# Grouped-query attention over a cache: reordering two pairs' outputs together, loading small rows of wo ahead of the last V block, and halving two loads of wo

## The chip, the cores and the metric

The kernel runs on one core of one Trainium2 chip. The metric is the time on the device in microseconds (us), as the median of several executions. Most executions of this program lie within 0.3 us of each other on a quiet chip. A *span* is the length of the one execution that the profiler recorded, from its first instruction to its last; it is a little shorter than the time. A run is called slow when it is over 1.5% above the fastest of the same kernel; verdicts use the other runs, called fast.

Engines are named as in the profile: PE (TensorE), DVE (VectorE), ACT (ScalarE), POOL (GpSimd), SP (the queue that issues the loads). A load *lands* when its data has arrived; the trace records sixteen landings for a full load, and a reader waits for the last of them. The *granted clock* is the share of PE's full clock that the profile shows as given to it.

## The reference, cut to what matters

```python
B, Sq, D = 8, 4, 512
Hq, Hkv, Sk, Dh = 32, 8, 2048, 128           # bf16 throughout
q = (x @ wq).reshape(B, Sq, Hq, Dh).transpose(0, 2, 1, 3)
k = repeat(k_cache, 4, axis=1); v = repeat(v_cache, 4, axis=1)
p = softmax(einsum("bhqd,bhkd->bhqk", q, k) * Dh ** -0.5)
o = einsum("bhqk,bhkd->bhqd", p, v)
return o.transpose(0, 2, 1, 3).reshape(B, Sq, Hq * Dh) @ wo
```

K and V are 32 MB each (in units of 1024 KB), wq and wo 4 MB each. Every byte is read once and used little, so the kernel is a stream of loads with matmuls beside it.

## The kernel before

The 8 heads of the cache are taken in four *pairs* (p = 0 to 3). A pair and a batch element make a *unit*: one K block and one V block of 1024 KB. All loads go through one queue in a fixed order, and the last ones are V block 31 and then most of wo:

```python
        if step == NH - 1 - 2 * VB:
            assert not loads                              # K and V are all issued
            nc.sync.dma_start(wo_n[:, :], wo[HP * 128 - 32 : HP * 128, :])   # 32 KB, pair 0
            load_wo_m()                                   # 512 KB, pair 0
            load_wo(1, 0, WR)                             # 1024 KB, pair 1
            load_wo(2, 0, WR)                             # 1024 KB, pair 2
            load_wo(3, 0, 4)                              # 512 KB, pair 3
            load_wo(3, 4, 2)                              # 256 KB
            load_wo(3, 6, 2)                              # 256 KB
```

The output of a pair lies with head dimension on partitions. To be multiplied by wo, it is turned in two steps, each (for pairs 1 to 3) of eight transposes on PE and an eviction, which is a copy of PE's result out of its psum tile, on DVE: `to_tokens(p)`, then `to_wo_rows(p)`. Pairs 0 to 2 are turned during the next pair's work; pair 3 can only be turned after V block 31. The end of the kernel is

```python
    to_tokens(3)
    project(0, 0, WM + 1)      # 10 matmuls of 256 columns
    to_wo_rows(3)
    project(1, 0, WR)          # 16 matmuls
    project(2, 0, WR)          # 16
    project(3, 0, 4)           # 8
    project(3, 4, 2)           # 4
    project(3, 6, 2)           # 4
    # ... ACT evicts half 0 of the output, DVE adds to half 1, two transfers store them
```

`project` runs over half 0 of the columns, then over half 1.

The softmax here doesn't subtract the row's maximum and nothing guards it: scores larger than these inputs give would overflow.

## Time and profile before

| | before |
|---|---|
| time, median (range, runs) | 189.90 us (189.82 to 190.06, 4) |
| span of the profiled execution | 187.7 us (its time was 189.51) |
| busy: PE, DVE, ACT | 85%, 61%, 46% of the span |
| share of the DMA engines' time in the queue of loads | 96.0% |
| read from memory | 75.53 MB, 403 GB/s over the span |

The lines that carry the argument stand in the prediction below. One more is the stretch of 1 us in which PE has nothing to do before the last V block lands (columns: stretch, its length, then busy time of PE, PE's weight loads, DVE, ACT and POOL with the number of instructions, the granted PE clock, the DMA share, GB/s).

```profile
174.00:175.00 1.00, 0.00 (x0) 0.00 (x0) 0.97 (x2) 0.00 (x0) 0.00 (x0) 1.00 1.04 426
```

PE is idle, DVE works on the norms of the last block, and the DMA engines are full.

### The profile page before, as it was taken

The page shows a single profiled execution, that of the slowest core. Times are in us where ns is not written, and L with a number is a line of the kernel's source. Part 1 is how long each engine was busy: PE and PEld are TensorE (multiplying, and loading weights), DVE is VectorE, ACT ScalarE, POOL GpSimd, SP SyncE. Part 2 cuts the span into 40 slices and gives each one's busy share as a digit, 9 for nine tenths or more (in the row PEclk, how much of TensorE's full clock was granted, in tenths as well). Part 3 has the DMA queues.
Part 4 walks back from the last instruction along what each step waited for, and adds up shares of the span by engine and source line. Part 5 has one row for each costly group of instructions (what it writes and reads, how often), then busy time and mean ns, then how long its engine had stood idle before and what let it go on. Part 6 is the DMA issues. An engine that isn't in the chain of part 4 may idle for free.

```text
span 187.7 us, 6524 instructions
## 1 busy us (share of the span) xinstructions
PE 159.3 (85%) x2931; PEld 142.2 (76%) x2931; DVE 113.7 (61%) x220; ACT 86.2 (46%) x170; POOL 6.3 (3%) x9
## 2 busy tenths in 40 slices
PE   0525697799999998999989999999888899999793
PEld 0515397699999898889877887899777789886482
DVE  0580544577777676767665666667666667667400
ACT  2012546665655664435545553546555544453000
POOL 8400000000000000000000000000000000000000
PEclk9995769999999999999999999999999999999999
DMA  6999999999999999999999999999999999999960
GB/s 209 461 447 382 423 436 418 429 425 426 420 424 421 419 431 421 419 436 419 422 429 421 424 429 419 424 421 428 424 424 426 422 428 424 421 429 417 413 271 8
DMA packets 10524, 75.99 MB, mean 405 GB/s; under 512 B 1240, under 2 KB 1368, under 8 KB 1880
## 3 DMA queue, kind: packets, MB, share of 16 engines
q1 hardware_dynamic: 10448, 75.55, 96.0%
q8 instruction: 23, 0.38, 0.7%
q14 instruction: 5, 0.04, 0.1%
q10 hardware_dynamic: 48, 0.02, 0.0%
HBM read 75.53 MB, written 0.03 MB: 403 GB/s over the span
## 4 chain that ended last, share of the span: by engine, by line
DMA 92%; issue 3%; PE 2%; POOL 0%; SPq 0%; DVE 0%; POOLq 0%
DMA k_sb<-in_k_cache_dram 62%; DMA wo_e<-in_wo_dram 13%; DMA wo_sb<-in_wo_dram 9%; DMA v_sb<-in_v_cache_dram 8%; PE out_e L371 1%; PE out_ps L371 1%; DVE out_sb L430 0%; SPq L107 0%; POOL ident masks.py:197 0%; POOL ident masks.py:199 0%; SPq L127 0%; POOL wo_e L164 0%; POOLq masks.py:199 0%; POOLq L447 0%
## 5 line engine op out<-in xcount | busy, mean ns | idle before, releaser
L188 PE MATMUL kp<-ident,k_sb 128*128 128x128 f32 x512 | 82.9, 288 | 14.6 <-POOL ident masks.py:199 7.0
L195 DVE COPY kt<-kp 128x1024 bf16<-128x1024 bf16 x96 | 65.2, 683 | 24.4 <-PE kp L188 23.9
L259 ACT ACTIVATE probs<-s_ps 64x256 bf16<-64x256 f32 x128 | 48.3, 378 | 66.6 <-PE s_ps L249 65.7
L188 PEld LDWEIGHTS kp<-ident,k_sb 128*128 128x128 f32 x512 | 55.9, 144 | 18.0 <-POOL ident masks.py:199 7.0
L249 PE MATMUL s_ps<-q_bd,kt 128*128 128x64 bf16 x1024 | 42.3, 194 | 3.0 <-ACT kt L193 1.9
L249 PEld LDWEIGHTS <-kt 128*128 128x128 bf16 x1024 | 39.9, 99 | 4.7 <-ACT kt L193 2.2
L273 PEld LDWEIGHTS <-v_sb 128*128 128x128 bf16 x1024 | 34.4, 96 | 9.4 <-DMA v_sb<-in_v_cache_dram 2.0
L193 ACT COPY kt<-kp 128x1024 bf16<-128x1024 bf16 x32 | 32.4, 1012 | 12.1 <-PE kp L188 11.4
L273 PE MATMUL o_ps<-probs,v_sb 128*128 128x32 bf16 x1024 | 35.0, 176 | 1.1 <-DMA v_sb<-in_v_cache_dram 1.0
L295 DVE TENSOR_REDUCE l_sb<-l_ps 128x32 f32<-128x512 f32 x32 | 22.1, 691 | 20.1 <-PE l_ps L287 20.0
L287 PE MATMUL l_ps<-probs,ones 128*128 128x512 bf16 x64 | 19.0, 379 | 0.0
L299 DVE RECIPROCAL r_sb<-l_sb 128x32 f32<-128x32 f32 x32 | 11.3, 353 | 1.1
L304 DVE TENSOR_TENSOR oT_all<-o_ps,r_sb 128x32 bf16<-128x32 f32 x32 | 5.8, 181 | 1.9 <-PE o_ps L273 1.6
L429 ACT CAST out_sb<-out_e 32x256 bf16<-32x256 f32 x1 | 0.4, 361 | 13.5 <-PE out_e L371 13.5
L287 PEld LDWEIGHTS <-ones 128*128 128x128 bf16 x64 | 6.1, 98 | 0.4
L236 DVE CAST q_bd<-pse 64x512 bf16<-64x512 f32 x4 | 2.6, 678 | 4.6 <-PE pse L227 4.6
L371 PEld LDWEIGHTS <-oP 128*32 128x32 bf16 x48 | 4.6, 97 | 1.0 <-issue 0.4
L164 POOL MEMSET wo_e<- 64x6144 bf16 x1 | 5.2, 5211 | 0.3 <-POOLq L447 0.3
L171 DVE COPY pick<-ident 128x64 bf16<-128x64 bf16 x4 | 0.6, 220 | 6.5 <-POOL ident masks.py:199 6.5
L356 PE MATMUL out_e<-wo_e,oE 64*32 64x256 bf16 x24 | 4.0, 272 | 0.0
L212 PE MATMUL psq<-xT_sb,wq_sb 128*128 128x32 bf16 x128 | 3.6, 188 | 0.3 <-DVE xT_sb L206 0.3
L212 PEld LDWEIGHTS <-wq_sb 128*128 128x128 bf16 x128 | 3.6, 104 | 0.3 <-issue 0.3
(43 smaller groups left out, 41.2 us busy)
## 6 DMA issues: line engine op xcount, KB each, us to landing
k_sb<-in_k_cache_dram SPq DMA_DIRECT2D x32, 1024.0 KB, 19.5
v_sb<-in_v_cache_dram SPq DMA_DIRECT2D x32, 1024.0 KB, 19.5
wq_sb<-in_wq_dram SPq DMA_DIRECT2D x1, 4096.0 KB, 14.3
wo_sb<-in_wo_dram SPq DMA_DIRECT2D x2, 1024.0 KB, 16.0
wo_m<-in_wo_dram SPq DMA_DIRECT2D x1, 512.0 KB
wo_sb<-in_wo_dram SPq DMA_DIRECT2D x1, 512.0 KB
wo_sb<-in_wo_dram SPq DMA_DIRECT2D x2, 256.0 KB
wo_e<-in_wo_dram SPq DMA_DIRECT2D x8, 60.0 KB
```

The source lines that it names most:

```text
L188: nc.tensor.transpose(kp[:, j, :], k4[:, w : w + 128], ident4[:, :])
L193: nc.scalar.copy(out=kt2, in_=kp2)
L195: nc.vector.tensor_copy(out=kt2, in_=kp2)
L212: nc.tensor.matmul(psq[:, h, :], lhsT=wq_sb[:, r, hh * 128 : (hh + 1) * 128], rhs=xT_sb[:, r, :], start=(r == 0), stop=(r == R - 1),)
L249: nc.tensor.matmul(s_ps[:, 2 * j : 2 * j + 2, :], lhsT=k_t[:, j % (HC // 4), :, e], rhs=q_bd[:, p, e, b, :, :], start=(e == 0), stop=(e == 1),
L259: nc.scalar.activation(out=pr[rows, hf * HC : (hf + 1) * HC, cols], in_=s_ps[rows, :, cols], func=EXP)
L273: nc.tensor.matmul(o_ps[u][:, :], lhsT=vs[u][:, cc, :], rhs=pr[:, cc, :], start=(cc == 0), stop=(cc == C - 1),)
L287: nc.tensor.matmul(l_ps[:, :, :], lhsT=ones[:, :], rhs=pr[:, c : c + LC, :], start=(c == 0), stop=(c + LC == C),)
L295: nc.vector.tensor_reduce(out=l_sb[:, :], in_=l_ps[:, :, :].rearrange("d c q -> d q c"), axis=AX, op=ADD)
L299: nc.vector.reciprocal(r_sb[:, :], l_sb[:, :])
L304: nc.vector.tensor_tensor(out=oT_all[:, p * HP : (p + 1) * HP, b, :], in0=o_ps[u][:, :].rearrange("d (h s) -> d h s", h=HP), in1=r_sbs[u][ ...
L371: nc.tensor.matmul(out_ps[half], lhsT=o, rhs=w[:, half * DH : (half + 1) * DH], start=(half == 1 and p == 0 and r == 0), stop=(p == G2 - 1 ...
```

## The change

Its intent is to shorten the end: PE should have less to do after the last V block, and start on the pieces of wo sooner. It has four parts.

1. Pairs 1 and 2 are turned together, once, instead of one after the other (64 rows instead of twice 32). Pair 0's turning loses some transposes too.
2. wo_n and wo_m, the last rows of pair 0, are loaded ahead of V block 31, and `project(0, ...)` runs three steps before the end.
3. Pairs 1 and 2 of wo are loaded and projected in halves.
4. `project` takes half 1 first, and DVE and ACT, with their stores, change order.

Core of the diff (cuts marked ...):

```diff
+        if u == NU + 2:
+            loads.append(("m", 0))                 # wo_n and wo_m, ahead of the last V block
...
     def project(p, r0, n):
-        for half in range(2):
+        for half in (1, 0):
...
-            elif p > 0 and b == 1:
-                to_tokens(p - 1)
-            elif p > 0 and b == 2:
-                to_wo_rows(p - 1)
+            elif p in (1, 3) and b == 1:
+                to_tokens(p // 2)                  # group 0: pair 0; group 1: pairs 1 and 2
+            elif p in (1, 3) and b == 2:
+                to_wo_rows(p // 2)
...
-            nc.sync.dma_start(wo_n[:, :], wo[HP * 128 - 32 : HP * 128, :])
-            load_wo_m()
-            load_wo(1, 0, WR)
-            load_wo(2, 0, WR)
+            load_wo(1, 0, 4)
+            load_wo(1, 4, 4)
+            load_wo(2, 0, 4)
+            load_wo(2, 4, 4)
...
+        if step == NH - 3:
+            out_ps = [...]
+            project(0, 0, WM + 1)
+
-    to_tokens(3)
-    project(0, 0, WM + 1)
-    to_wo_rows(3)
-    project(1, 0, WR)
-    project(2, 0, WR)
+    to_tokens(2)                                   # group 2: pair 3
+    project(1, 0, 4)
+    to_wo_rows(2)
+    project(1, 4, 4)
+    project(2, 0, 4)
+    project(2, 4, 4)
...
+    nc.vector.tensor_tensor(out=out_sb[1][:, :], in0=out_ps[1], in1=early[:, :], op=ADD)
     nc.scalar.copy(out=out_sb[0][:, :], in_=out_ps[0])
-    nc.vector.tensor_tensor(out=out_sb[1][:, :], in0=out_ps[1], in1=early[:, :], op=ADD)
+    nc.sync.dma_start(out=o2[:, DH:], in_=out_sb[1][:, :])
     nc.scalar.dma_start(out=o2[:, :DH], in_=out_sb[0][:, :])
-    nc.sync.dma_start(out=o2[:, DH:], in_=out_sb[1][:, :])
```

More of the change, by code (lines that the diff above doesn't have):

```diff
@@ L85 @@
     ident4 = const.tile([128, 128], FP32, name="ident4")
-    oT_all = const.tile([128, Hq, B, Sq], BF16, name="oT_all")
+    groups = [(0,), (1, 2), (3,)]
+    oT = [const.tile([128, HP, len(ps), B, Sq], BF16, name=f"oT{ps[0]}") for ps in groups]
     out_sb = [const.tile([T, DH], BF16, name=f"out_sb{i}") for i in range(2)]
-    oP = [None] + [const.tile([128, WR, T], BF16, name=f"oP{p}") for p in range(1, G2)]
+    oP12 = const.tile([128, WR, 2, T], BF16, name="oP12")
+    nat_sb = const.tile([2 * T, HP * 128 + 288], BF16, name="nat_sb")
+    oP3 = const.tile([128, WR, T], BF16, name="oP3")
+    oP = [None, oP12[:, :, 0, :], oP12[:, :, 1, :], oP3[:, :, :]]
     oE = const.tile([64, WE, T], BF16, name="oE")
@@ L94 @@
     ones = const.tile([128, 128], BF16, name="ones")
-    pad = const.tile([128, 96], BF16, name="pad")
+    pad = const.tile([128, 64], BF16, name="pad")
     probs = [const.tile([128, C, NQ], BF16, name=f"probs{i}") for i in range(L // 2 + 2)]
@@ L129, in load_wo_m @@
     def load_wo_m():
+        nc.sync.dma_start(wo_n[:, :], wo[HP * 128 - 32 : HP * 128, :])
         nc.sync.dma_start(
@@ L154, in load_ready @@
             kind, u = loads[-1]
-            if kind == "e":
+            if kind in "em":
                 loads.pop()
-                load_wo_e(u)
+                load_wo_e(u) if kind == "e" else load_wo_m()
                 continue
@@ L223 @@
         )
-    for p in range(G2):
-        pse = psum_s.tile([128, 2, B, NQ], FP32, tag="s", name="pse")
+    for pp in range(0, G2, 2):
         for e in range(2):
+            pse = psum_s.tile([128, 2, B, NQ], FP32, tag="s", name="pse")
             nc.tensor.matmul(
-                pse[:, e, :, :],
+                pse[:, :, :, :],
                 lhsT=pick[:, e, :, :],
-                rhs=qT_all[:, p, :, :, :].rearrange("d b h s -> d (b h s)"),
+                rhs=qT_all[:, pp : pp + 2, :, :, :].rearrange("d p b h s -> d (p b h s)"),
                 start=True,
@@ L233 @@
             )
-        for g in range(2):
-            rows = slice(g * 64, (g + 1) * 64)
-            (nc.scalar.copy if g else nc.vector.tensor_copy)(
-                out=q_bd[rows, p, :, :, g, :], in_=pse[rows, :, :, :]
-            )
+            for g in range(2):
+                rows = slice(g * 64, (g + 1) * 64)
+                (nc.scalar.copy if g else nc.vector.tensor_copy)(
+                    out=q_bd[rows, pp : pp + 2, e, :, g, :], in_=pse[rows, :, :, :]
+                )
     wo_sb = wpool.tile([128, G2 - 1, WR, D], BF16, tag="w", name="wo_sb")
@@ L304, in finish @@
         nc.vector.tensor_tensor(
-            out=oT_all[:, p * HP : (p + 1) * HP, b, :],
+            out=oT[(p + 1) // 2][:, :, (p == 2) * 1, b, :],
             in0=o_ps[u][:, :].rearrange("d (h s) -> d h s", h=HP),
@@ L311, with to_tokens @@
     nats = {}
-    def to_tokens(p):
-        nat = psum_l.tile([T, HP, 128], BF16, tag="l", name="nat")
+    def to_tokens(n):
+        rows = len(groups[n]) * T
+        nat = psum_l.tile([rows, HP, 128], BF16, tag="l", name="nat")
         for h in range(HP):
             nc.tensor.transpose(
-                nat[:, h, :],
-                oT_all[:, p * HP + h, :, :].rearrange("d b s -> d (b s)"),
-                ident[:, :],
-            )
-        nat_sb = small.tile([T, HP * 128 // WR, WR], BF16, tag="nat_sb", name="nat_sb")
+                nat[:, h, :], oT[n][:, h, :, :, :].rearrange("d p b s -> d (p b s)"), ident[:, :]
+            )
+        flat = nat[:, :, :].rearrange("t h d -> t (h d)")
+        nats[n] = nat_sb[:rows, : HP * 128 + (n == 0) * 288]
+        if n > 0:
+            nc.vector.tensor_copy(out=nats[n][:, :], in_=flat)
+            return
+        w = 32 * WE
+        nc.vector.tensor_copy(out=nats[0][:, :w], in_=flat[:, :w])
@@ L322, in to_tokens @@
         nc.vector.tensor_copy(
-            out=nat_sb[:, :, :].rearrange("t q r -> t (q r)"),
-            in_=nat[:, :, :].rearrange("t h d -> t (h d)"),
-        )
-        nats[p] = nat_sb
-    def to_wo_rows(p):
-        flat = nats[p][:, :, :].rearrange("t q r -> t (q r)")
-        if p > 0:
-            perm = psum_l.tile([128, WR, T], BF16, tag="l", name="perm")
-            rows = flat.rearrange("t (q r) -> t r q", r=WR)
+            out=nats[0][:, w : 2 * w], in_=flat[:, NE // 2 * WE : NE // 2 * WE + w]
+        )
@@ L333, in to_wo_rows @@
+        nc.vector.tensor_copy(out=nats[0][:, 2 * w :], in_=flat[:, NE * WE :])
+    def to_wo_rows(n):
+        rows = len(groups[n]) * T
+        if n > 0:
+            perm = psum_l.tile([128, WR, rows], BF16, tag="l", name="perm")
+            by_row = nats[n][:, :].rearrange("t (q r) -> t r q", r=WR)
             for r in range(WR):
-                nc.tensor.transpose(perm[:, r, :], rows[:, r, :], ident[:T, :T])
-            nc.vector.tensor_copy(out=oP[p][:, :, :], in_=perm[:, :, :])
+                nc.tensor.transpose(perm[:, r, :], by_row[:, r, :], ident[:rows, :rows])
+            to = oP3[:, :, :] if n == 2 else oP12[:, :, :, :].rearrange("q r p t -> q r (p t)")
+            nc.vector.tensor_copy(out=to, in_=perm[:, :, :])
@@ L336, in to_wo_rows @@
             return
         perm = psum_l.tile([128, WE + WM + 1, T], BF16, tag="l", name="perm")
-        rows = flat[:, : NE * WE + 12 * WE].rearrange("t (q r) -> t r q", r=WE)
+        w = 64 * WE
+        by_row = nats[0][:, :w].rearrange("t (q r) -> t r q", r=WE)
         for r in range(WE):
-            for hi in range(2):
-                q0 = hi * NE // 2
-                nc.tensor.transpose(
-                    perm[hi * 32 : hi * 32 + 32, r, :], rows[:, r, q0 : q0 + 32], ident[:T, :T]
-                )
@@ L346, in to_wo_rows @@
-        rows = flat[:, NE * WE : HP * 128 - 32].rearrange("t (q r) -> t r q", r=WM)
+            nc.tensor.transpose(perm[:64, r, :], by_row[:, r, :], ident[:T, :T])
+        by_row = nats[0][:, w : w + 128 * WM].rearrange("t (q r) -> t r q", r=WM)
         for r in range(WM):
-            nc.tensor.transpose(perm[:, WE + r, :], rows[:, r, :], ident[:T, :T])
-        nc.tensor.transpose(perm[:32, WE + WM, :], flat[:, HP * 128 - 32 :], ident[:T, :T])
+            nc.tensor.transpose(perm[:, WE + r, :], by_row[:, r, :], ident[:T, :T])
@@ L350, in to_wo_rows @@
+        nc.tensor.transpose(perm[:32, WE + WM, :], nats[0][:, w + 128 * WM :], ident[:T, :T])
         nc.vector.tensor_copy(out=oN[:, :], in_=perm[:32, WE + WM, :])
@@ L364, in project @@
     def project(p, r0, n):
-        for half in range(2):
+        for half in (1, 0):
             for r in range(r0, r0 + n):
                 if p > 0:
-                    o, w = oP[p][:, r, :], wo_sb[:, p - 1, r]
+                    o, w = oP[p][:, r], wo_sb[:, p - 1, r]
                 else:
@@ L417 @@
             nc.vector.tensor_copy(out=early[:, :], in_=out_e[:, 1, :])
-    out_ps = [out_e[:, 0, :], psum_s.tile([T, DH], FP32, tag="s", name="out_ps")[:, :]]
-    to_tokens(3)
-    project(0, 0, WM + 1)
-    to_wo_rows(3)
-    project(1, 0, WR)
-    project(2, 0, WR)
+        if step == NH - 3:
+            out_ps = [out_e[:, 0, :], psum_s.tile([T, DH], FP32, tag="s", name="out_ps")[:, :]]
+            project(0, 0, WM + 1)
[5 more added lines that the diff above has]
+    project(2, 4, 4)
     project(3, 0, 4)
```

## The prediction

> **What bounds the kernel now.** I read the page's slices first, to see which resource is full and where it stops being full.
>
> ```profile
> PE   0525697799999998999989999999888899999793
> DMA  6999999999999999999999999999999999999960
> GB/s 209 461 447 382 423 436 418 429 425 426 420 424 421 419 431 421 419 436 419 422 429 421 424 429 419 424 421 428 424 424 426 422 428 424 421 429 417 413 271 8
> ```
>
> From the second slice to the 38th the DMA engines are full at about 424 GB/s, whatever the compute engines do. 75.5 MB must be read from memory, and 75.5 MB / 424 GB/s is 178 us of the 187.7 us span. So work on TensorE (PE) or VectorE (DVE) that is taken out of the middle is worth nothing; only the stretch in which the DMA row falls, the last 5% of the span, can pay. Next I read the chain of work that ended last, from the place where it enters that stretch:
>
> ```profile
> 165.00 16.04 DMA wo_sb<-in_wo_dram
> 181.04 0.04 issue
> 181.08 1.03 PE out_e L371 x8
> 182.12 0.87 PE out_ps L371 x8
> 182.99 0.44 PE out_e L371 x4
> 183.43 0.44 PE out_ps L371 x4
> 183.86 0.22 PE out_e L371 x2
> 184.08 0.22 PE out_ps L371 x2
> 184.30 0.22 PE out_e L371 x2
> 184.52 0.23 PE out_ps L371 x2
> 184.75 0.02 issue
> 184.77 0.41 DVE out_sb L430
> ```
>
> The chain leaves the DMA at 181.04, when pair 2's quarter of wo, one transfer of 1024 KB, has landed whole. From there PE runs 32 matmuls without a pause until 184.75. Three smaller pieces of pair 3 landed meanwhile and no wait shows for them: PE was behind. The 32 matmuls start between 181.08 and 184.55, so one takes 3.47/32 = 0.1085 us in the stream (the 0.27 us that a record shows is its latency). Last I read busy time and DMA share by stretches of 1 us, to see when data really ends (columns: stretch, its length, five engines busy, granted clock, DMA share, GB/s):
>
> ```profile
> 177.00:178.00 1.00, 1.00 (x9) 0.61 (x9) 0.59 (x1) 0.00 (x0) 0.00 (x0) 1.00 1.03 428
> 178.00:179.00 1.00, 1.00 (x13) 0.76 (x11) 0.00 (x0) 0.00 (x0) 0.00 (x0) 1.00 0.81 340
> 181.00:182.00 1.00, 0.92 (x9) 0.81 (x9) 0.00 (x0) 0.00 (x0) 0.00 (x0) 1.00 0.66 256
> 182.00:183.00 1.00, 1.00 (x12) 0.89 (x10) 0.00 (x0) 0.00 (x0) 0.00 (x0) 1.00 0.39 137
> 183.00:184.00 1.00, 1.00 (x11) 0.89 (x10) 0.00 (x0) 0.00 (x0) 0.00 (x0) 1.00 0.02 6
> ```
>
> Some DMA engines run dry at 178 (share 0.81, 13 of 16), the slowest near 183.6, so the finish is uneven. The trace also records the sixteen landings of every transfer. I group them by transfer and take the last of each: block 30 of V at 172.44, block 31 (the last) at 174.99, wo_n 175.20, wo_m 176.24, pair 1 at 178.63, pair 2 at 181.06, and pair 3's pieces (512, 256, 256 KB) at 182.33, 182.97 and 183.59. All are on one queue in this order.
>
> **What the Trainium skill says.**
> 1. "DMA: Bandwidth & Descriptors", "Why a DMA increments its semaphore by 16 and not by 1": a transfer is spread over up to 16 engines that finish independently, and only the full count means that all has landed. The trace agrees: the last piece's sixteen landings run from 178.31 to 183.59, and pair 2's 16 matmuls start at 181.08, after its last landing at 181.06. So a reader waits for the slowest engine on the whole transfer, and halving a transfer lets half the reading start earlier.
> 2. Same page, "Measured (HBM→SBUF, 128 partitions, SWDGE, issued from GpSimd)": 1 MB alone gets 78% of peak, and its rule asks for 1 MiB or more. That speaks against halves. It is for transfers by themselves on another issue path; behind one another on a full queue this trace shows no such cost. Averaged over the sixteen engines, 1024 KB (pair 2) took 2.44 us after the transfer before it, 512 KB 1.22, and the 256 KB pieces 0.63 each.
> 3. "TensorE: Matmul & The Clock Gate", "Back-to-back issue gap": N/2.4 + 2.5 ns warm, for N = 256 that is 109 ns. The trace's 108.5 ns agrees, so this tail already runs at PE's rate, with the granted clock at 1.00, and can be shortened only by starting earlier.
>
> **The change part by part.**
> *Pairs 1 and 2 reordered together.* The order of instructions in both kernels shows 32 fewer matmul instructions in the changed one: 16 transposes (two groups of 8 go), 12 in pair 0's reordering (one transpose in place of two for each of 12 rows), and 4 matmuls of 512 columns in place of 8 of 256 in the setup. At 0.1 us or so that is about 3 us of PE. All of it lies before 160 us, where the DMA share is 1.01 in the stretches of 40 us that I read: 0 on the path. Two VectorE evictions go, and pair 0's copy becomes three: also 0.
>
> *Rows of pair 0 (wo_n, wo_m) ahead of the last V block.* 32 + 512 KB on the queue take 176.24 - 174.99 = 1.25 us. The last V block therefore lands at 176.24 instead of 174.99, and nothing behind it moves. Pair 0's 10 projection matmuls, which lay at 176.8 to 178.3 between the last V block and the end, now run in the pause in which PE waited for that block (PE busy 0.00 from 174 to 175). They wait for wo_m (172.44 + 1.25 = 173.69) and take about 1.1: done at 174.8. Then the last block's sums (0.5) to 175.3, reduction and reciprocal (0.69 + 0.35) to 176.4, in time for the V matmuls (176.25 + 0.96 = 177.2). Scaling (0.19) to 177.4, eight transposes (0.6) to 178.05, eviction (0.68) to 178.8. PE spends that eviction on half of pair 1 (landed near 177.4; 8 x 0.1085 = 0.87) to 178.9, then eight reordering transposes (0.6) to 179.5.
>
> *Halves of pairs 1 and 2.* Estimated landings from the rates above: 177.4, 178.6, 179.85, 181.06. PE does the second half of pair 1 from 179.5 to 180.4, the first of pair 2 to 181.2, the second to 182.1. It has caught up 0.2 us before the first piece of pair 3 lands at 182.33. From there 16 matmuls remain instead of 32: 182.35 + 16 x 0.1085 = 184.09 in place of 181.08 + 3.47 = 184.55. **PE ends 0.47 us earlier**, at about 184.28. The later pieces (182.97, 183.59) land before PE reaches them at 183.2 and 183.65.
>
> *Halves of the output swapped.* Before, the path ended with the 0.41 us VectorE addition on the half that finished last. Now that half finishes first, and a 0.36 us ScalarE copy ends the path: 0.05 us. Both output transfers show about 1.45 us from issue to their last landing, so swapping their queues gives nothing.
>
> Sum: 0.47 + 0.05 = 0.52 us. Two more transfers cost a little; the 256 KB pieces took 0.63 where a quarter of 2.44 would be 0.61, so 0.02 each, 0.04 together. Net gain 0.48, and the time 189.85 - 0.5 = **189.3 us**.
>
> **The rivals.**
> (a) *Hidden anyway.* Pair 0's early projection and the shorter reordering could give nothing, since PE waits for pair 2 at 181.04 as things stand. True for those two parts alone: the idle 0.26 us before 181.08 says that PE had slack there. Only the halves turn that slack into time. If PE does not catch up before 182.33, the gain shrinks by as much as it is late; my slack is 0.2 us. Time then 189.4 to 189.8.
> (b) *A new wait.* The last V block is 1.25 us later, and its scaling, transposes and reordering hang on it. Pair 3 needs them at 182.33; reordering ends at 179.5 and its 0.29 us eviction before 180. Over 2 us to spare, so I give this little. If it bound, the time would be 190 or more.
> (c) *The DMA becomes slower.* Halves read 4 KB runs in place of 8 KB, and eight transfers in flight now carry fewer bytes. The transfer queue issued the last piece at 172.43, when V block 30 had landed (eight transfers earlier); now it must wait for wo_m near 173.7. The fastest DMA engine reached the last piece at 177.7, so it is not starved. At 5% on 2 MB it would be 0.25 us: 189.55.
> (d) *PE as the bound in the middle.* The page has PE at 85% and 32 fewer instructions would then help by up to 3 us (187). The full DMA row speaks against it.
>
> **Range and chances.** The three runs before span 0.13 us. The gain is at most 182.33 to 181.06, less what PE needs to catch up, and (a) and (c) can take nearly all of it; a chance shift of the slowest DMA engine is worth some tenths either way. I take 188.9 to 189.7. A change of 2% is 3.8 us, over the whole tail behind the last landing (187.7 - 183.6 = 4.1 us): 1% for each side, 98% within.
>
> **What would show it.** In the changed profile: DMA share about 1.0 to 178 us and the same uneven fall; the last landing within 0.2 us of 183.6; the 10 matmuls of pair 0 before the last V block, that block near 176.2; PE waiting briefly for pair 3's first piece and the chain leaving the DMA there, near 182.3, with 16 matmuls behind it; PE ending near 184.3; the ScalarE copy as last step. It is wrong if the last landing moves by over 0.3 us, if PE shows no wait before pair 3's first piece, or if a new wait for the reordering stands there.

## The result, and the profile after

| | before | after |
|---|---|---|
| time, median (range, runs) | 189.90 us (189.82 to 190.06, 4) | 189.32 us (189.28 to 189.78, 4) |
| ratio | | 0.9974, 95% interval 0.9957 to 0.9991 |
| span of the profiled execution | 187.7 us | 187.5 us |
| last landing of wo | 183.56 us | 183.94 us |
| from there to the end of the span | 4.14 us | 3.56 us |

A ratio is the mean time of one kernel's fast runs over that of the other's fast runs of the same rounds, so not quite the ratio of the medians. The landing is the last of the sixteen that the trace records for the last piece of wo, put on the profile's clock by an instruction that both show (the prediction has the same landing as 183.59). Spans are printed to 0.1 us, so a length up to the end of the span, here and in the table below, is good to 0.05 us only.

The change is 0.6 us, 0.3%, and clear of the noise on that chip, but within 2%. The profile after, read in the order of before, first the DMA row and the rate in 40 slices:

```profile
DMA  6998999999999999999999999999999999999970
GB/s 204 467 447 377 422 429 426 420 428 426 422 418 430 423 419 423 432 419 428 421 423 428 425 423 426 423 418 428 423 428 426 419 428 419 428 422 418 411 292 13
```

The stream is as it was, full to the 38th slice. Next the end of the chain that ended last (start, length, what):

```profile
172.75 9.91 DMA wo_sb<-in_wo_dram
182.66 0.04 issue
182.71 0.60 PE out_ps L382 x4
183.30 0.44 PE out_e L382 x4
183.74 0.22 PE out_ps L382 x2
183.96 0.22 PE out_e L382 x2
184.18 0.22 PE out_ps L382 x2
184.39 0.23 PE out_e L382 x2
184.63 0.02 issue
184.65 0.36 ACT out_sb L445
```

The chain now leaves the DMA at 182.66, where pair 3's first piece lands, and not at pair 2. 16 matmuls follow instead of 32, and the ACT copy is last. Last, two stretches of 1 us:

```profile
174.00:175.00 1.00, 0.99 (x9) 0.61 (x9) 0.18 (x1) 0.00 (x0) 0.00 (x0) 1.00 0.97 401
182.00:183.00 1.00, 0.82 (x8) 0.57 (x7) 0.00 (x0) 0.00 (x0) 0.00 (x0) 1.00 0.35 133
```

Pair 0's projection fills the pause from 174 to 175 (0.99 busy, 0.00 before), and at 182 PE has a little slack: it is waiting for data again.

### The profile page after: what moved, and what is told of

Its sections match the earlier page's. It is cut to its first block, busy times and chain, and to the rows that moved or that the text cites. A ratio compares the mean times of both kernels' runs of the same rounds, so it can differ in the third digit from the quotient of the medians.

```text
span 187.5 us, 6432 instructions
## 1 busy us (share of the span) xinstructions
PE 157.3 (84%) x2869; PEld 141.2 (75%) x2899; DVE 113.2 (60%) x220; ACT 86.3 (46%) x170; POOL 6.3 (3%) x9
## 4 chain that ended last, share of the span: by engine, by line
DMA 91%; issue 3%; PE 2%; SPq 1%; POOL 0%; ACT 0%; POOLq 0%
DMA k_sb<-in_k_cache_dram 60%; DMA v_sb<-in_v_cache_dram 19%; DMA wo_e<-in_wo_dram 7%; DMA wo_sb<-in_wo_dram 5%; PE kp L196 1%; PE out_ps L382 1%; SPq L132 0%; PE out_e L382 0%; SPq L112 0%; PE s_ps L257 0%; PE o_ps L281 0%; ACT out_sb L445 0%; POOL ident masks.py:197 0%; POOL ident masks.py:199 0%; POOL wo_e L172 0%
## 5 line engine op out<-in xcount | busy, mean ns | idle before, releaser
L295 PE MATMUL l_ps<-probs,ones 128*128 128x512 bf16 x34 | 12.6, 379 | 1.5
L312 DVE TENSOR_TENSOR oT<-o_ps,r_sb 128x32 bf16<-128x32 f32 x32 | 5.8, 182 | 1.4 <-PE o_ps L281 1.2
L382 PE MATMUL out_ps<-wo_sb,oP 128*32 128x256 bf16 x24 | 3.8, 273 | 0.2 <-DMA wo_sb<-in_wo_dram 0.2
```

What stands on the lines that cost most here:

```text
L295: nc.tensor.matmul(l_ps[:, :, :], lhsT=ones[:, :], rhs=pr[:, c : c + LC, :], start=(c == 0), stop=(c + LC == C),)
L312: nc.vector.tensor_tensor(out=oT[(p + 1) // 2][:, :, (p == 2) * 1, b, :], in0=o_ps[u][:, :].rearrange("d (h s) -> d h s", h=HP), in1=r_sbs ...
L382: nc.tensor.matmul(out_ps[half], lhsT=o, rhs=w[:, half * DH : (half + 1) * DH], start=(half == 1 and p == 0 and r == 0), stop=(p == G2 - 1 ...
```

## The experiments

The question is which part carries the 0.6 us. Theory H: the halves do, because they let PE catch up before pair 3 lands. Theory E: the early rows and the common turning do, because they take work from the end.

The twelve runs were made on three chips (a, b and c). There the kernel before itself took 189.63 to 196.08 us (33 runs), so the intervals of the ratios reach 0.6 to 0.9% either way and can't resolve 0.3%. I therefore use two things beside the medians: the lowest times (of 6 runs, against 11 of the kernel before, which favours the latter), and a length inside one trace, from the last landing of wo to the end of the span, which doesn't depend on how fast the stream was before. It agreed within 0.1 us wherever one kernel had several profiles with the clock at 1.00 in the end.

| run | chip | lowest, median us | profile | last landing | PE's last result | landing to end of span |
|---|---|---|---|---|---|---|
| before | first | 189.82, 189.90 | fast | 183.56 | 184.75 | 4.14 |
| aa_before | a | 189.98, 191.62 | fast | 183.96 | 185.22 | 4.24 |
| after | first | 189.28, 189.32 | fast | 183.94 | 184.63 | 3.56 |
| after_again | b | 189.18, 189.77 | fast | 184.02 | 184.71 | 3.58 |
| after_c | c | 189.33, 189.84 | fast | 184.43 | 185.15 | 3.57 |
| no_halves | a | 189.69, 191.50 | fast | 184.95 | 186.22 | 4.25 |
| no_halves_b | b | 189.97, 191.29 | fast | 184.30 | 185.57 | 4.20 |
| halves_only | a | 189.32, 191.27 | slow | 188.82 | 192.35 | 6.48 |
| halves_b | b | 189.17, 190.46 | slow | 187.02 | 187.72 | 3.58 |
| halves_c | c | 189.40, 191.59 | slow | 187.80 | 191.07 | 6.20 |
| halves_fine | c | 189.12, 191.82 | fast | 184.02 | 184.57 | 3.38 |
| fine_tail | b | 189.04, 189.35 | fast | 184.07 | 184.51 | 3.33 |
| fine_tail_b | c | 188.82, 189.14 | fast | 183.96 | 184.40 | 3.34 |
| spread_e7 | a | 190.52, 191.21 | fast | 185.21 | 185.93 | 3.49 |

The kernel before had a lowest time of 189.70 on chip a, 189.63 on b and 189.75 on c. All runs gave correct results.

### The kernel before, again: aa_before

No edit.

> The kernel before, unchanged, as a control. Expected: ratio 1.000 within 0.001. Its profile is a second look at the last landing of wo (183.57 us in the first) and at the time at which the last V block lands (174.97); if these move by 0.3 us between two looks at the same kernel, the 0.36 us by which they are later in the changed kernel's profile is chance and no cost of the change.

The ratio was 1.002, but with an interval from 0.9935 to 1.0104: the chip was too restless for the control to be worth 0.1%. The trace was of use. The last landing came at 183.96 us, 0.40 us later than in the first look at the same kernel, and the whole end moved with it:

```profile
165.36 16.15 DMA wo_sb<-in_wo_dram
181.51 0.04 issue
181.55 1.03 PE out_e L371 x8
```

The wait for pair 2 ends at 181.51 instead of 181.04. So the 0.38 us by which the stream ended later in the changed kernel's profile is what two looks at one kernel differ by; it is no proof of a cost.

### The changed kernel, again: after_again, after_c

No edit of the changed kernel.

> The changed kernel once more, beside the others on the same chip, because the first call fell on a chip where the kernel before itself scattered from 189.7 to 196.1 us. Expected: ratio 0.9975 within 0.001 if the chip is quiet; in the profile, whatever the last landing is, PE waits for the first piece of pair 3 and has 16 matmuls left.

> The changed kernel, as the measure for the other three of this call. So far its profiles show 3.56 and 3.58 us from the last landing of wo to the end of the span, against 4.14 and 4.24 for the kernel before. Expected again: 3.57 within 0.05, and ratio 0.997.

The ratios were 0.9937 (0.9869 to 1.0004) and 0.9958 (0.9882 to 1.0034): on the right side, and too wide to say more. The length from the last landing to the end was 3.58 and 3.57 us, as in the first profile, though the last landing itself came at 184.02 and 184.43. These are the measures for the runs beside them.

### All but the halves: no_halves, no_halves_b

```diff
-            load_wo(1, 0, 4)
-            load_wo(1, 4, 4)
-            load_wo(2, 0, 4)
-            load_wo(2, 4, 4)
+            load_wo(1, 0, WR)
+            load_wo(2, 0, WR)
...
-    project(1, 0, 4)
     to_wo_rows(2)
-    project(1, 4, 4)
-    project(2, 0, 4)
-    project(2, 4, 4)
+    project(1, 0, WR)
+    project(2, 0, WR)
```

> The changed kernel without the halves. My theory: PE is again waiting for the whole of pair 2 and has 32 matmuls left, so 0 to 0.1 us less than before, ratio 0.9995 to 1.0. Rival (the other parts carry the gain): 0.4 us or more less, ratio below 0.998.

> All but the halves, again. My theory: 0 to 0.1 us less than before, ratio 0.9995 to 1.0 (the last V block is 1.25 us later and PE has 1.2 us less to do behind it, so PE runs without a pause into the 48 last matmuls at the same time as before). Rival (these parts carry the gain): ratio below 0.998.

The ratios were 1.0001 and 1.0008, each with an interval of 0.8% either way; the lowest times, 189.69 and 189.97, are at or above those of before on the same chips (189.70, 189.63). The length from the last landing to the end was 4.25 and 4.20 us, as before the change. Theory E falls, in this form. The number came as expected, but not for the reason that I gave: I had PE waiting for the whole of pair 2 again, and neither trace shows such a wait. The chain of no_halves_b says why taking work from the end gave nothing:

```profile
178.81 0.69 DVE nat_sb L331
179.50 0.05 issue
179.54 0.67 PE perm L347 x8
180.21 0.98 PE out_ps L382 x8
181.19 0.87 PE out_e L382 x8
182.06 0.87 PE out_ps L382 x8
182.94 0.87 PE out_e L382 x8
```

The path no longer goes through a landing of wo here but through DVE's eviction of 0.69 us between the two turnings of pair 3. Before, pair 0's projection covered that eviction. With it gone PE stood idle, 0.78 us before the second turning in the trace of no_halves, and then ran all 48 remaining matmuls with no wait. The edit also takes away the half of pair 1 that the changed kernel puts there, so early rows with the hole filled by other work were not tried.

### The halves alone: halves_only, halves_b, halves_c

The same kernel three times: the one before, with

```diff
-            load_wo(1, 0, WR)
-            load_wo(2, 0, WR)
+            load_wo(1, 0, 4)
+            load_wo(1, 4, 4)
+            load_wo(2, 0, 4)
+            load_wo(2, 4, 4)
...
-    project(1, 0, WR)
-    project(2, 0, WR)
+    project(1, 0, 4)
+    project(1, 4, 4)
+    project(2, 0, 4)
+    project(2, 4, 4)
```

> The kernel before with one part of the change: pairs 1 and 2 of wo loaded and projected in halves. My theory (PE starts on pair 2 earlier and has 16 instead of 32 matmuls left after its last wait): 0.45 us less, ratio 0.9976, the chain leaves the DMA at the first piece of pair 3. Rival (the gain comes from the shorter reordering and the early rows, the halves are paid for by the DMA): within 0.1 us of before.

> Halves alone, again. My theory (halves carry the gain): 0.44 us less than before, ratio 0.9977, PE without a pause from about 178.9 us on, since pair 0's projection still lies behind the last V block. Rival (early rows are needed too, because without them PE has 1.2 us more to do after the last V block and can't catch up): 0.1 to 0.2 us less only, ratio 0.9990 to 0.9995.

> Halves alone, a third time, because both earlier profiles fell in the slow state. My theory (the halves are the whole gain): last landing to end 3.55 to 3.65 us in a fast run, time as the changed kernel within 0.1 us. Rival (early rows or the shorter reordering are part of it): 3.8 us or more, and 0.2 us or more behind the changed kernel.

The ratios were 0.9959, 0.9967 and 0.9979, all with intervals that hold 1; that the halves carry the gain rests on the traces. The lowest times (189.32, 189.17, 189.40) stand where the changed kernel's do (189.18, 189.33) and 0.35 to 0.46 us under those of before on the same chips. All three profiles fell in the slow state. In halves_b, whose clock stayed at 1.00 in the end, the length from last landing to end was 3.58 us, that of the changed kernel; in the other two it was 6.48 and 6.20, because the PE clock fell (see the last section but one). A fast look at this order of work came with the next run.

### Halves and five pieces for pair 3, without the other parts: halves_fine

halves_only, and in addition

```diff
-            load_wo(3, 0, 4)
-            load_wo(3, 4, 2)
-            load_wo(3, 6, 2)
+            load_wo(3, 0, 2)
+            load_wo(3, 2, 2)
+            load_wo(3, 4, 2)
+            load_wo(3, 6, 1)
+            load_wo(3, 7, 1)
```

with `project` cut likewise.

> The kernel before with halves and with pair 3 in five pieces, but without the early rows and the shorter reordering. Theory that the early rows buy PE slack which only finer pieces can use: PE runs without a pause behind the last V block (its 48 last matmuls started at 178.9 and need 5.2 us), so finer pieces give nothing here, 3.55 to 3.65 us from the last landing to the end, as halves alone. Rival (the early rows are worth nothing at all): 3.33 us, as the changed kernel with five pieces.

The ratio was 1.0001 (0.9921 to 1.0082): two of its six runs took 189.1 us and four 191.7 to 191.9. The timeline of its end (start, length, engine, line, operation; in brackets the idle time before it and what ended that), from the last V block on:

```profile
175.25 0.96 PE L273 MATMUL o_ps<-probs,v_sb 128*128 128x32 bf16 x32 [1.00 <-DMA v_sb<-in_v_cache_dram]
179.14 0.61 PE L371 MATMUL out_e<-wo_sb,oP 128*32 128x256 bf16 x4
184.28 0.27 PE L371 MATMUL out_ps<-wo_sb,oP 128*32 128x256 bf16 x1
184.59 0.41 DVE L438 TENSOR_TENSOR out_sb<-out_ps,early 32x256 bf16<-32x256 f32 x1 [5.05 <-PE out_ps L371]
```

PE starts the 48 matmuls at 179.14 and never waits again. From the start of the last V block's matmuls to PE's last result it took 184.57 - 175.25 = 9.32 us; the kernel before took 184.75 - 175.01 = 9.74 in its fast profile, and 9.79 in aa_before. The difference, 0.42 us and more, is the pause before pair 2 that halves remove. halves_b took 187.72 - 178.39 = 9.33, so finer pieces gave PE nothing here, as expected: it was already running without a pause. My expectation of 3.55 to 3.65 us from last landing to end still missed (3.38), and the rival's 3.33 lies nearer. With no wait left, that length is set by how late the last landing is against PE, not by work behind the landing: from the start of the V block's matmuls to the last landing it took 184.02 - 175.25 = 8.77 us here and 187.02 - 178.39 = 8.63 in halves_b. It was the wrong measure for a chain that doesn't pass through the landing, so whether the early rows are worth anything beside finer pieces (3.33 in fine_tail, 3.38 here) was not settled.

### Five pieces for pair 3 in the changed kernel: fine_tail, fine_tail_b

The edit of halves_fine, made in the changed kernel.

> The changed kernel with pair 3 of wo in five pieces of 2, 2, 2, 1 and 1 rows per partition in place of 4, 2 and 2. In the changed kernel PE had 16 matmuls left at its last wait (182.66) and ended 0.7 us after the last landing (183.93 to 184.63). If PE follows the landings, two matmuls and the latency are left after the last one (0.22 + 0.2): 0.25 us less than the changed kernel, less 0.04 for two more transfers, ratio to before 0.9964. Rival (PE is already paced by its own matmuls, or the extra transfers cost more): same as the changed kernel, 0.9975.

> The changed kernel with pair 3 in five pieces, again, for its time against the changed kernel in the same rounds. Expected: 3.33 us from the last landing to the end (measured before), 0.2 us less time than the changed kernel, ratio to before 0.996.

Lengths 3.33 and 3.34 us, against 3.56 to 3.58: 0.23 us, as expected. The medians are 0.42 and 0.70 us below the changed kernel's in the same rounds (189.35 against 189.77, 189.14 against 189.84), more than the 0.2 expected, but the changed kernel scatters more there. The ratios to before, 0.9923 (0.9863 to 0.9983) and 0.9907 (0.9833 to 0.9980), lie below 1, inflated by restless runs of the kernel before. The end of the chain in fine_tail:

```profile
183.52 0.31 PE out_ps L382 x2
183.83 0.22 PE out_e L382 x2
184.05 0.11 PE out_ps L382
184.16 0.11 PE out_e L382
184.26 0.12 PE out_ps L382
184.38 0.12 PE out_e L382
184.53 0.36 ACT out_sb L449
```

Two matmuls are left after the last landing at 184.07, so PE ends 0.44 us after it, 0.22 for them and 0.2 for latency. Little is left to gain behind the landing on PE. Its ratio to the kernel before is below 1; against the changed kernel it was faster in both medians and both lowest times, but no interval was worked out for that pair, and either gain is far within 2%.

### Spreading one load over all DMA engines: spread_e7

In the changed kernel, the last of eight small loads for pair 0 (five rows of 12 KB) was made row by row, each viewed as 16 x 384 elements:

```diff
+        if i == 7:
+            for t in range(0, 17, 4):
+                nc.sync.dma_start(
+                    wo_e[a + t : a + t + 1, :, :].rearrange(...).rearrange("p (n k) -> p n k", n=16),
+                    rows[b + t : b + t + 1, :, :].rearrange(...).rearrange("p (n k) -> p n k", n=16))
+            return
```

> The changed kernel with the last five rows of wo_e (60 KB) loaded one by one, each spread over sixteen DMA engines instead of one engine per row. Theory that the slowest DMA engine sets the end: in the trace the five engines that carry wo_e are 3.5 us behind after it, and the very last landing is one of theirs; 12 KB less on each is 0.45 us earlier, 3.75 KB more on all is 0.14 us later, so the last landing and the time fall by 0.3 us against the changed kernel (ratio to before 0.996). Rival (the sum of bytes sets the end, or the five small transfers take places in the queue and starve it): same as the changed kernel, 0.9974, or slower.

Ratio 1.0013 (0.9930 to 1.0095), lowest 190.52: slower if anything. The experiment did not do what it was made for. Each of the five rows has a single landing in the trace, 0.6 to 1.1 us after the one before, and is still one packet of 12 KB, so one DMA engine carried them in turn. And the five small loads took five of eight places in flight. SP, which issues a load only when the one eight places earlier has landed, was held from 34.7 to 43.1 us, and the stream fell to 359 GB/s in the tenth slice. The rival had the queue starve. But from 44 to 52 us stretches of 2 us show 283 to 395 GB/s at a DMA share of 0.93 to 1.00, and the mean 8 KB packet took 0.33 to 0.43 us in them instead of 0.31: the engines were slow rather than idle, and why stays open. The landings of the last piece lay 4.5 us apart (180.7 to 185.2) and 5.5 in the changed kernel (178.4 to 183.9), so the slowest engine came nearer to the rest, but later by the clock; whether relieving it pays stays open.

## Why the prediction was right or wrong

The time was forecast at 189.3 us and measured at 189.32, within the range of 188.9 to 189.7. So close a hit is luck: the four runs lie between 189.28 and 189.78, and the forecast's own sum, 189.85 - 0.48 = 189.37, was rounded down. Point by point:

- *The DMA bounds the middle, PE work removed there gives 0.* Right: the stream is full in both profiles, and the common turning gave nothing together with the early rows (no_halves 4.20 and 4.25 us behind the last landing, before 4.14 and 4.24). It was not run apart from them.
- *PE leaves the DMA at pair 3's first piece with 16 matmuls left.* Right: 182.66, then 16 matmuls to 184.63. The step was forecast to take 184.28 - 182.33 = 1.95 us, and took 1.97.
- *PE catches up 0.2 us before that piece.* Right in kind, and with more to spare: the matmuls of pair 2's second half begin at 181.49, so by 0.1085 us each they were through at 182.36, 0.3 us before 182.66. (The working has small slips that change nothing: 184.55 is where the ACT copy starts, and the last of the 32 matmuls starts at 184.46, 31 steps of 0.109 us after the first; 184.55 - 184.09 is 0.46.)
- *Pair 0's projection runs in the pause before the last V block, and that block lands near 176.24.* Right: PE busy 0.99 from 174 to 175, and the block's matmuls at 176.47.
- *The ACT copy is last.* Right, 0.36 us. Swapping the halves was not timed alone. From PE's last result to the end of the span the traces have, to 0.01 us, 2.98 and 2.99 in the two looks at the kernel before and 2.97 and 2.96 in no_halves and no_halves_b, which have the swap; with the halves it is 2.91 without the swap (halves_b) and 2.90 with it (the changed kernel). So the 0.05 us claimed for the swap doesn't show.
- *The last landing within 0.2 us of 183.6.* Wrong: 183.94, and with it every later absolute time by 0.3 to 0.4. The prediction had named a move of over 0.3 us as a sign that it is wrong, and by its own test that sign came (0.38). The same shift shows in aa_before, 0.40 us with nothing changed, so the limit was tighter than what two looks at one kernel differ by. The forecast of the time did not suffer, because it took the gain from 189.85, the median of the three runs of before then known, and not from the profiled execution, which was faster than all of them (189.51).
- *Two more transfers cost 0.04 us.* Mis-sized as a term. Packets of 8192 bytes took a mean of 0.3116 us in the trace before, those of 4096 bytes 0.160 in the trace after. One of the sixteen DMA engines moves 128 KB of pairs 1 and 2: 16 x 0.3116 = 4.99 us, or 32 x 0.160 = 5.12, so about 0.13 us is the estimate. It is smaller than the scatter of the last landing and was not seen in the time.
- *Gain 0.48 us.* Measured 0.58 in the medians and 0.58 behind the last landing (4.14 to 3.56). Of the latter, 0.50 is PE's last result coming nearer to the last landing (1.19 us behind it before, 0.69 after), where 0.47 was forecast; the rest, 0.08, lies behind PE's last result, where the swap doesn't account for it, and stays unexplained.
- *Rival (a), parts 1 and 2 hidden anyway and only the halves turn slack into time:* shown by no_halves and, for PE's path in a fast profile, by halves_fine; not by a ratio, since no ratio of the halves alone is clear of 1. What I had not seen is that the early rows open a hole at the eviction of pair 3, which half of pair 1 has to fill.
- *Rivals (b) and (d)* did not occur: pair 3's turning was done before it was needed, and the middle stayed bound by the stream.

## What to carry to other kernels

In a kernel bound by loads, look at the work that waits for the last few transfers, not at busy shares: cutting a transfer that the consumer waits for whole is worth at most that wait (0.42 us here), and only where the consumer stays behind from there to the end. Work moved out of the tail gives nothing by itself if it was covering something else there; check what becomes idle. And when a chip scatters by several per cent, a length inside one trace, between two events that the change lies between, still resolves a tenth of a microsecond, as long as the path runs through both.

## What the runs showed that I had not expected

**The clock at the end.** In two of the three profiles of the halves alone the PE clock fell to one half for 6.8 us right at the end, from 181.7 and 180.1 us on. The stretches of 2 us of halves_c:

```profile
182.00:184.00 2.00, 2.00 (x11) 0.83 (x10) 0.00 (x1) 0.00 (x0) 0.00 (x0) 0.50 0.87 349
184.00:186.00 2.00, 2.00 (x16) 1.52 (x15) 0.29 (x1) 0.00 (x0) 0.00 (x0) 0.50 0.79 307
```

The matmuls took twice their time, and landing to end 6.20 us. PE had paused for 1.12 us before the last V block. No profile of a kernel with the early rows, which fill that pause, showed such a fall near the end. On chips b and c 12 of 22 runs of the kernel before took over 191.7 us, 3 of 12 of the changed one and 1 of 12 of fine_tail; but so did 2 of 6 of no_halves_b, which has the early rows too. That may be a second use of the early rows, but it is not shown: both profiles are of slow runs, and halves_b was slow with a full clock, by a stream that ended late. Nor does the length of the pause decide: aa_before paused for 1.11 us at the same place and kept its clock, halves_only for 1.10 and lost it. And the early rows don't keep the clock up elsewhere: in fine_tail, a fast profile, it fell to one half for 3.4 us from 83.4 us on,

```profile
84.00:86.00 2.00, 2.00 (x30) 1.94 (x28) 0.86 (x3) 0.76 (x2) 0.00 (x0) 0.50 1.00 422
```

though PE's longest pause between 70 and 88 us was 0.39 us. What makes the clock fall, and these runs slow, stays open.

**Instructions share the stream, and small loads stagger it.** The trace before has 23 packets of 16 KB in a queue of kind instruction, each taking about 0.9 us, one every 7 us or so. Near such moments one of the sixteen landings of the next block falls back, mostly by 1.4 to 1.7 us, against the rest. They are not the main reason why the sixteen landings of the last piece lie 5.3 us apart (178.3 to 183.6 us). The trace has that distance at 0.4 us for the K block that lands at 18.0 us and at 3.7 us for the one at 50.5. Between them it grows in steps of about 0.46 us, while the eight small loads for pair 0 (five rows each) are on the queue; each of their rows is one packet of 12 KB, which took 0.46 us. Two later steps of 0.9 us, to 4.6 at 53.9 and to 5.4 at 125.9, are as long as one instruction packet each. This is argued from sizes and times that agree; no run took either kind away.

## What the Trainium skill lacked or had wrong

- "DMA: Bandwidth & Descriptors", "Measured (HBM→SBUF, 128 partitions, SWDGE, issued from GpSimd)": it has times by size of a transfer and a rule of 1 MiB or more, and no section of the page compares runs of 4 KB and 8 KB in a stream of loads on this chip. Behind one another on a full queue, cutting 8 KB runs into 4 KB runs cost 2.7% per byte (0.3116 us for 8192 bytes against twice 0.160), and halving two loads of 1024 KB shortened PE's path behind the last V block by 0.42 us.
- "Runtime: NRT & Kernel Launch", "Instruction fetch mechanics": it calls the cost of crossing a 16 KiB boundary mostly hidden, which is about the engine that runs the instructions, and it does not say what the loads lose. In this kernel, bound by loads, each packet of 16 KB took about 0.9 us of one DMA engine, 23 times (0.7% of the engines' time).
- "TensorE: Matmul & The Clock Gate", "HAM oscillation — how this bites in real kernels": its rule is no PE gap over about 3.4 us. Here the clock fell to 0.50 for 3.4 us in a fast profile in which PE paused for at most 0.39 us in the 13 us before (fine_tail, at 83.4 us), and for 6.8 us after a gap of 1.12 us in a slow one (halves_c), while a gap of 1.11 us left it at 1.00 (aa_before).
